# Moving about 400 pieces of a hand-ordered FNet and feed-forward kernel to other places

## The chip, the cores and the metric

The kernel runs on one core of a Trainium2 chip. The time is the device time of one execution in microseconds; smaller is better. The engines are PE (TensorE, matmuls), DVE (VectorE), ACT (ScalarE), POOL (GpSimd) and SP (SyncE, which here only issues DMAs).

## The reference

An FNet mixing layer and a feed-forward layer, each behind a layer norm, over x of 2048 rows and 512 columns in fp32:

```python
def _A_ref(x, dft_seq_re, dft_seq_im, dft_hid_re, dft_hid_im):
    a = jnp.einsum("bsd,ed->bse", x, dft_hid_re)
    b = jnp.einsum("bsd,ed->bse", x, dft_hid_im)
    return jnp.einsum("ts,bse->bte", dft_seq_re, a) - jnp.einsum("ts,bse->bte", dft_seq_im, b)
...
h = x + _A_ref(_layernorm(x, axis=-1), A_dft_seq_re, A_dft_seq_im, A_dft_hid_re, A_dft_hid_im)
h2 = h + _B_ref(_layernorm(h, axis=-1), B_w1, B_w2)
```

where `_B_ref` is `silu(x @ w1) @ w2` with 1792 hidden features.

## The kernel before

**Arithmetic.** Every fp32 product is three matmuls in the fp32r type (`three`, L285 to L287): an operand v is split into a rounded part (`rounded`, L235: an ACT copy to fp32r, names ending in h) and a remainder (L239 and L241: a DVE subtraction, names ending in l). In the tables, `ph` and `pl` are the parts of a page `raw` of the DFT matrix, `S` and `X` those of sums of the normalized x and of x itself, `gth` and `gtl` those of the activations. Large products are done by seven block products instead of eight, so that many block sums are made on DVE, and many banks of PSUM are emptied by ACT copies (`copy_out`: `C` at L536, `p` at L650).

**Stages.** `plain(0, 0)`, `fast(1, 0)`, `mix(0)` make the mixing layer for one half of the output rows, `fast(0, 1)`, `fast(1, 1)`, `mix_fast(1)` for the other; `up` and `down` are the two products of the feed-forward layer. A column sum over all partitions, needed for the second layer norm, is POOL's `partition_all_reduce` (`total`, L952 to L954), eight times in all, each behind two DVE sums of its own; `m01` is one of its results. One kind of block sum over `raw` is made by an accumulating DMA that POOL issues (L702).

**The end.** `down` closes with output blocks `r00`, `r01`, `r10`, `r11` (128 x 1024 each), to which banks of PSUM are added (`add`, L1245) before SP stores them (`store`, L1211). The last two banks are `f5`, added to `r01` and `r11`, and `f4`, of which the first half is added to one half of `r10`; the other half of `r10` was put into bank `f4b` beforehand (L1263), where PE's last matmuls add to it, and is copied out in two pieces, one by DVE (L1287) and one by ACT (L1285), stored by SP and by ACT's own queue (L1288).

**The order.** The program is a list of 1477 events, small functions that issue a few instructions. Each has a place in microseconds, given by `step` and `at` with leads and delays by hand; `program()` adds to the place of event n the number `MOVED[n]`, and sorts:

```python
return sorted(((t + MOVED.get(n, 0.0), at, n, f) for t, at, n, f in events), key=lambda v: v[:3])
```

The kernel issues the events in that order, and on PE, DVE, ACT, POOL and SP each instruction stays behind the one issued before it (`issue_after`, `ORDERED`). So an instruction whose input is late holds up all that stands behind it on its engine. The places are not times at which anything runs; they give only the order. A `Plan` replays the same list ahead and hands out 51 SBUF pages by the order of their last uses, so that another order also gives other pages, and with them other waits of a load for the page that it overwrites.

Of the kernel before, what the change touches and what calls it, by code (L numbers as in the profile page):

```python
# [44 lines left out]
    0: -52.37, 1: -33.2, 2: -38.66, 3: -18.04, 4: -26.92, 5: -20.32, 6: -29.82, 7: -14.98, 8: -9.18, 11: -10.08,  # L45
    12: 25.37, 14: 18.68, 16: 23.49, 21: 2.24, 24: 5.1, 28: 5.71, 31: -2.34, 32: -4.51, 35: 4.85, 36: 5.08, 38: -0.24,
    39: 3.5, 40: 11.88, 41: 1.55, 42: 0.25, 46: 6.79, 53: -4.31, 54: 1.45, 58: -0.74, 59: -9.01, 60: -6.33, 61: -8.84,
    64: -6, 65: -1.09, 66: -2.09, 67: -5.31, 68: -4.92, 71: -10.71, 72: -9.91, 73: -3.53, 74: -2.8, 78: 3.78,
    79: 6.06, 80: 0.77, 81: -13.68, 82: 4.24, 84: -30.43, 85: -17.16, 86: -25.23, 87: -17.93, 88: 2.24, 89: 1.74,
    93: 2.98, 95: -6.14, 96: -2.42, 98: -1.97, 99: -7.61, 100: -1.63, 102: -5.02, 107: -16.33, 110: -10.38,  # L50
    111: -25.35, 112: -9.3, 118: -5.99, 119: -1.79, 122: 1.43, 123: 4.1, 126: -10.19, 127: 0.73, 129: 5.4, 130: 4.42,
    131: -3.95, 134: 0.06, 135: 2.84, 137: -2.02, 139: 1.11, 141: -5.61, 142: 1.4, 145: 2.5, 146: 4.5, 147: 4.57,
    148: 4.6, 149: 3.43, 150: 2.26, 151: 19.19, 152: -7.18, 153: -6.63, 155: 11.15, 156: 11.07, 157: 9.78, 158: 12.14,
    159: 13.16, 160: 16.93, 161: 13.96, 162: -2.9, 163: -3.39, 164: -1.57, 165: -14.91, 166: -17.14, 167: -1.43,
    168: -0.32, 169: -3.29, 170: -12.4, 171: -5.05, 172: -32.94, 173: -31.77, 174: -8.22, 175: -4.04, 176: -5.26,
    179: 0.15, 180: 10.12, 181: 15.11, 182: -25.4, 183: -2.31, 184: -4.6, 186: 1.11, 188: 8.91, 189: 8.76, 190: 7.03,
    191: 5.95, 192: -10.95, 193: -3.24, 194: -7.1, 195: -6.25, 196: -9.27, 197: -18.74, 198: -8.3, 199: -9.45,
    200: -10.15, 201: -10.15, 202: 23.62, 203: 13.92, 204: 13.22, 205: 13.48, 206: 15.71, 207: -25.16, 208: -5.87,
    209: -6.45, 211: -30.57, 212: 4.81, 213: 5.94, 215: 3.47, 216: 4.56, 217: 7.05, 219: -16.42, 221: 2.26,
    223: 10.17, 224: -6.48, 225: -5.63, 226: -3.21, 228: -3.03, 229: 1.98, 233: 6.23, 234: 4.63, 236: -20.67,  # L60
    237: -4.86, 238: -2.92, 240: 13.91, 241: -7.64, 242: -0.78, 243: -2.11, 245: -18.15, 246: 1.78, 247: 1.56,
    249: -6.13, 250: -0.11, 251: 4.03, 253: 7.26, 254: 3.79, 255: 5.2, 257: 2.94, 258: 6.21, 259: 5.94, 260: -5.32,
    261: 0.52, 262: 2.64, 263: -4.66, 265: 4.76, 266: 3.32, 268: 4.67, 269: 3.04, 271: 8.94, 272: 7.88, 273: 0.53,
    274: 5.4, 275: 11.11, 276: -4.5, 278: 7.7, 279: 5.88, 280: 15.06, 282: -4.98, 283: -3.67, 285: -6.12, 286: 0.9,
    288: 2.33, 289: 2.31, 290: 2.16, 291: 2.6, 292: 2.43, 293: -5.69, 295: 6.59, 296: 5.2, 297: 6.85, 299: -1.02,
    302: -1.88, 303: 5.15, 306: 1.26, 307: -5.64, 308: 2.53, 309: 1.36, 310: -1.13, 312: 7.01, 313: 2.51, 314: 3.71,
    315: 2.32, 317: 2.86, 318: 4.16, 320: 2.57, 321: 1.08, 322: 2.71, 324: 2.35, 325: 6.97, 326: 6.39, 327: 7.74,
    329: 2.18, 330: -17.05, 331: -10.08, 332: -6.68, 335: -4.49, 338: 4.22, 339: 6.54, 341: -20.61, 342: -9.19,
    343: 5.09, 344: 5.24, 345: 6.04, 346: 4.03, 347: 2.51, 349: -6.51, 350: -8.89, 351: -7.77, 352: -0.77, 353: 4.15,
    354: -8.39, 355: 4.62, 356: 5.31, 357: 3.14, 358: 1.71, 360: -8.8, 361: -4.61, 362: 0.81, 363: -0.42, 364: 2.41,  # L70
    365: 2.61, 367: -19.81, 368: -19.31, 370: -9.58, 371: -3.37, 372: 3.24, 373: 1.07, 374: 5.51, 375: 6.78,
    376: 13.95, 378: 8.17, 379: 12.62, 380: -2.37, 381: -4.43, 382: -5.31, 383: 9.92, 384: 12.54, 385: -5.3,
    386: 10.75, 387: 3.35, 388: 4.44, 389: 1.23, 392: 31.21, 393: -1.74, 394: -4.65, 395: -5.49, 396: 2.12, 397: 0.45,
    399: 0.6, 400: -4.78, 401: 3.37, 402: -1.34, 403: 3.45, 404: 11.63, 405: 8.49, 406: 2.76, 407: 6.66, 408: -10.79,
    409: -5.26, 410: -16.78, 411: -4.87, 412: -19.75, 413: -6.46, 416: 8.66, 417: 7.28, 418: 6.58, 419: 15.43,
    420: 11.64, 421: 16.66, 422: -28, 423: -3.82, 424: 0.47, 427: 5.11, 428: 6.96, 430: -5.76, 431: -3.41, 432: -4.29,
    434: -24.87, 435: -5.1, 436: 5.45, 439: -3.5, 441: 3.31, 444: 5.76, 445: 3.6, 447: -10.22, 448: 2.95, 449: 2.53,
    451: 1.94, 452: 3.93, 453: 5.93, 455: 11.48, 456: -5.77, 457: 6.32, 458: 6.74, 460: 10.61, 461: 4.86, 462: 6.27,
    464: 5.91, 465: 9.22, 466: 7.05, 468: 0.59, 469: 3.35, 470: 4.72, 474: -1.83, 475: -1.07, 478: -2.17, 480: 1.69,
    481: -0.48, 484: 6, 486: 4.72, 487: 3.83, 488: 5.34, 489: 4.77, 490: 5.95, 491: 5.71, 493: 7.13, 494: 5.75,  # L80
    495: -3.07, 497: 5.65, 498: 5.03, 500: 5.02, 501: 3.02, 503: 5.25, 504: 4.47, 505: 0.13, 506: 1.52, 507: 2.32,
    510: 6.63, 511: 5.94, 512: 11.03, 514: 5.45, 515: 5.04, 517: -0.39, 518: -1.83, 520: 3.53, 521: 1.36, 522: 5.69,
    523: 4.52, 524: 5.7, 525: 2.14, 527: 8.59, 528: 7.15, 529: 5.77, 530: 7.7, 536: 1.31, 539: 9.45, 540: 6.62,
    541: 6.7, 542: 8.33, 544: 9.12, 545: -33.8, 546: 4.76, 547: 1.6, 548: 16.35, 549: -27.35, 550: -9.59, 551: -11.76,
    554: 4.38, 555: 4.21, 558: 3.97, 559: 4.8, 562: 0.83, 563: 3.82, 566: 5.9, 567: 4.31, 568: 4.51, 570: -20.73,
    571: -14.98, 572: -9.8, 575: 2.87, 576: 0.73, 578: -26.34, 579: -16.65, 580: -12.12, 582: 12.19, 583: 5.44,
    584: 2.64, 585: 4.63, 587: -12.47, 589: 2.94, 591: -3.53, 592: -5.23, 593: -2.61, 596: 6.89, 597: 5.63, 600: 5.72,
    601: 3.55, 602: -6.54, 603: -2.43, 604: -1.51, 605: -5.19, 607: -7.33, 608: 6.06, 610: -7.3, 614: 4.59, 615: -5.2,
    616: -5.83, 618: -8.39, 620: 8.96, 621: 7.18, 622: 6.56, 624: 6.01, 625: 3.84, 627: -8.97, 628: 5.64, 632: -4.62,
    633: -5.73, 634: -5.8, 635: -9.76, 637: 6.54, 638: 5.49, 639: 1.47, 642: 3.21, 644: -10.88, 645: -9.35,  # L90
    647: -3.63, 648: -5.58, 649: -12.3, 650: -1.4, 651: -2.57, 652: -19.86, 654: 3.38, 655: 3.83, 656: 6.13,
    659: -10.23, 660: 5, 664: 7.28, 666: 2.38, 668: 4.1, 669: 3.47, 672: -17.88, 673: -27.63, 674: -23.93,
    675: -34.26, 676: -10.49, 678: -14.8, 680: -19.6, 681: -10.83, 683: 4.38, 684: -18.81, 685: 18.83, 687: 1.39,
    688: -0.78, 692: -19.67, 693: -16.11, 694: -13.42, 695: 36.58, 697: 4.07, 698: 4.26, 699: 2.87, 701: 13.95,
    702: 16.83, 703: -4.89, 704: 0.12, 705: -7.59, 706: 0.42, 709: 1.31, 710: -32.96, 713: 26.35, 714: -20.76,
    716: -30.12, 717: -7.52, 719: -2.44, 723: 15.38, 724: -16.97, 728: 5.47, 730: 1.07, 731: 10.4, 732: -3.37,
    733: -0.27, 738: 12.29, 739: 13.87, 740: -42.3, 741: -31.4, 743: 2.11, 746: 4.55, 747: 9.34, 748: 16.67,
    749: 13.34, 750: 20.58, 751: 26.94, 752: 17.9, 753: 22.79, 754: 22.53, 755: 21.55, 756: 21.49, 757: 19.02,
    758: 47, 759: 32.53, 760: 38.11, 761: 39.91, 762: 13.17, 763: 13.96, 764: 16.64, 765: 14.1, 766: 18.58,
    767: 16.64, 768: 11.21, 769: 10.58, 770: 16.25, 771: 13.78, 772: 14.65, 773: 42.57, 774: 29.6, 775: 38.6,  # L100
    777: 5.55, 778: 2.68, 779: 3.67, 780: 2.46, 781: 3.5, 782: 6.91, 783: 22.33, 784: 13.98, 785: 12.14, 786: 12.92,
    787: 18.89, 788: 18.92, 789: 21.01, 790: -23.55, 791: -25.77, 792: 3.41, 793: 1.24, 794: -10.65, 795: -1.97,
    796: 22.62, 797: -5.44, 799: 40.61, 800: 41.64, 801: 29.18, 802: 27.1, 803: 38.77, 804: -41.83, 805: -21.78,
# [1310 lines left out]
```

## Time and profile before

| | us |
|---|---|
| median of 3 runs (lowest, highest) | 677.45 (677.36, 677.74) |
| the profiled execution | 678.98 |
| its span | 677.2 |
| outside its span | 1.8 |
| PE busy in the span | 665.1 (98%) |
| DVE / ACT / POOL busy | 574.9 / 365.3 / 99.5 |
| mean granted TensorE clock | 0.997 |

The profile is one execution. A row of its timeline gives the start, the duration, the engine, the line, the operation, the tiles and, in brackets, how long the engine had been idle just before and what it waited for. Matmuls overlap, so that a matmul of 0.39 us may follow the one before it after 0.23; the distance between two starts, less that pitch, is what PE lost between them. Rows of the view of waits give an engine and line, whom it waited for, and the microseconds in total, the count and the longest.

### The profile page before, as it was taken

How to read it: one execution, taken by the hardware profiler on the slowest of the kernel's cores; microseconds unless marked ns; L12 is line 12 of the kernel's file. 1: busy time of each engine (PE TensorE's matmuls, PEld its weight loads, DVE VectorE, ACT ScalarE, POOL GpSimd, SP SyncE). 2: the span in 40 equal slices, each digit the busy share in tenths (PEclk: the TensorE clock that was granted, in tenths of full speed). 3: DMA queues.
4: the chain of work that ended last, by engine and by line, in shares of the span. 5: the costliest groups of instructions: out<-in, count | busy, mean ns of one | idle time of the engine just before them, and what ended most of it. 6: DMA issues, size and time to landing. Idle time of an engine off the chain costs nothing.

```text
span 677.2 us, 8341 instructions
## 1 busy us (share of the span) xinstructions
PE 665.1 (98%) x2916; PEld 545.8 (81%) x2916; DVE 574.9 (85%) x723; ACT 365.3 (54%) x459; POOL 99.5 (15%) x130
## 2 busy tenths in 40 slices
PE   8999999999999999999999999999999999999996
PEld 5887887888888778888888888888888888888884
DVE  7999999798767899899989997978989765579864
ACT  6979556463444353544554645676544655565500
POOL 0021201112121251213120002442010000000000
PEclk9999999999999999999999999999999999999998
DMA  8978999779699888789999999727998845878602
GB/s 311 394 236 219 291 390 315 240 214 310 233 362 384 308 279 248 224 283 369 321 298 346 389 325 363 276 92 221 328 417 300 348 139 181 310 278 304 226 31 94
DMA packets 61786, 189.59 MB, mean 280 GB/s; under 512 B 6960, under 2 KB 14640, under 8 KB 61744
## 3 DMA queue, kind: packets, MB, share of 16 engines
q1 hardware_dynamic: 46608, 136.33, 56.6%
q0 software_dynamic: 14848, 52.46, 24.2%
q8 instruction: 23, 0.38, 0.2%
q10 hardware_dynamic: 288, 0.26, 0.1%
q14 instruction: 19, 0.16, 0.1%
HBM read 142.88 MB, written 46.15 MB: 279 GB/s over the span
## 4 chain that ended last, share of the span: by engine, by line
PE 85%; DVE 7%; DMA 3%; ACT 3%; issue 1%; DVEq 0%; SPq 0%; ACTq 0%
PE m L286 10%; PE m L285 10%; PE m L287 10%; PE y L285 8%; PE y L287 8%; PE y L286 8%; PE f L287 6%; PE f L285 6%; PE f L286 6%; PE vx L287 3%; PE vx L286 3%; PE vx L285 3%; DVE pl L239 2%; DMA raw<-in_seq 2%; PE c L285 2%; PE c L286 2%
## 5 line engine op out<-in xcount | busy, mean ns | idle before, releaser
L235 ACT ACTIVATE ph<-raw 128x1024 fp32r<-128x1024 f32 x102 | 104.9, 1055 | 88.2 <-DMA raw<-in_seq 16.8
L239 DVE TENSOR_TENSOR pl<-raw,ph 128x1024 fp32r<-128x1024 f32 x92 | 112.4, 1242 | 11.4 <-ACT ph L235 10.6
L286 PE MATMUL m<-pl,S 128*128 128x512 f32 x192 | 75.0, 390 | 0.0
L287 PE MATMUL m<-ph,S 128*128 128x512 f32 x192 | 74.8, 390 | 0.0
L285 PE MATMUL m<-ph,S 128*128 128x512 f32 x192 | 74.8, 389 | 0.0
L285 PE MATMUL f<-gth,wf 128*128 128x512 f32 x161 | 62.7, 389 | 0.0
L287 PE MATMUL f<-gth,wf 128*128 128x512 f32 x161 | 62.7, 389 | 0.0
L286 PE MATMUL f<-gtl,wf 128*128 128x512 f32 x161 | 62.7, 389 | 0.0
L235 ACT ACTIVATE gth<-g 128x1024 fp32r<-128x1024 f32 x42 | 43.3, 1053 | 30.5 <-DVE g L1230 26.5
L239 DVE TENSOR_TENSOR gtl<-g,gth 128x1024 fp32r<-128x1024 f32 x42 | 50.8, 1220 | 10.2 <-ACT gth L235 10.1
L286 PE MATMUL m<-pl,X 128*128 128x512 f32 x144 | 56.4, 392 | 1.3 <-DVE pl L239 1.3
L285 PE MATMUL m<-ph,X 128*128 128x512 f32 x144 | 56.2, 391 | 1.3 <-ACT p L650 1.3
L287 PE MATMUL m<-ph,X 128*128 128x512 f32 x144 | 56.1, 390 | 0.0
L1113 DVE TENSOR_TENSOR g<-vx,g 128x512 f32<-128x512 f32 x42 | 28.8, 687 | 30.3 <-PE vx L287 13.6
L687 DVE TENSOR_TENSOR raw<-raw,raw 128x1024 f32<-128x1024 f32 x36 | 47.7, 1331 | 0.7 <-DMA raw<-in_seq 0.4
L286 PEld LDWEIGHTS m<-pl,S 128*128 128x128 f32 x192 | 36.0, 188 | 7.9 <-DVE pl L239 0.5
L285 PEld LDWEIGHTS m<-ph,S 128*128 128x128 f32 x192 | 36.1, 188 | 7.5
L287 PEld LDWEIGHTS m<-ph,S 128*128 128x128 f32 x192 | 36.0, 188 | 7.4
L1110 ACT ACTIVATE g<-y 128x512 f32<-128x512 f32 x42 | 25.0, 596 | 27.7 <-PE y L287 27.7
L1107 ACT ACTIVATE g<-g 128x512 f32<-128x512 f32 x42 | 26.1, 627 | 17.9 <-DVE g L1113 17.9
L286 PEld LDWEIGHTS f<-gtl,wf 128*128 128x128 f32 x161 | 30.2, 188 | 6.3
L285 PEld LDWEIGHTS f<-gth,wf 128*128 128x128 f32 x161 | 30.2, 188 | 6.2
(334 smaller groups left out, 1582.8 us busy)
## 6 DMA issues: line engine op xcount, KB each, us to landing
raw<-in_seq SPq DMA_DIRECT2D x84, 512.0 KB, 6.1
wf<-wd SPq DMA_DIRECT2D x56, 512.0 KB, 5.6
sf<-sd SPq DMA_DIRECT2D x28, 512.0 KB, 6.3
raw<-in_seq POOLq DMA_DIRECT2D x16, 512.0 KB, 7.2
w<-in_ffn SPq DMA_DIRECT2D x28, 256.0 KB, 7.7
hf<-fd SPq DMA_DIRECT2D x12, 512.0 KB, 6.4
c<-cd SPq DMA_DIRECT2D x8, 512.0 KB, 7.6
h<-in_xT SPq DMA_DIRECT2D x8, 512.0 KB, 7.8
```

Of the source, the lines that this page charges most:

```text
L235: nc.scalar.activation(hi, src, AF.Copy, scale=sign)
L239: nc.vector.tensor_tensor(lo, src, hi, op=ALU.subtract)
L285: nc.tensor.matmul(acc, wh, mh, start=first, stop=False, skip_group_check=on)
L286: nc.tensor.matmul(acc, wh, ml, start=False, stop=False, skip_group_check=on)
L287: nc.tensor.matmul(acc, wl, mh, start=False, stop=last, skip_group_check=on)
L687: nc.vector.tensor_tensor(o, a, b, op=ALU.subtract)
L1107: nc.scalar.activation(g[q, f][:, tau, :], src, AF.Silu)
L1110: nc.scalar.activation(g[q, f][:, tau, :], src, AF.Copy)
L1113: nc.vector.tensor_tensor(g[q, f][:, tau, :], src, g[q, f][:, tau, :], op=ALU.add)
```

## The change

Only the table `MOVED` is another: 378 of its entries are new, gone or changed. The computation and the instructions of each engine are the same ones. The new table is seven lines longer, so that all that follows stands seven lines further down in the changed kernel (L1245 is L1252 there). PE's order stays but for one step of the first stage; on DVE 190 of 720 instructions move by more than three places, 29 by more than fifteen; on ACT 72 of 459 by more than three; on POOL four; on SP, 55 of 305.

```diff
 MOVED = {
...
-    1485: 17.39, 1499: 35.62,
+    1441: -21.66, 1485: 17.39, 1497: 35.87, 1499: 43,
 }
```

**The end, on DVE.** Before, the adds of `r01` and `r11` stand behind the copy from `f4b`:

```order
L1245 TENSOR_TENSOR r11_5348<-r11_5348,p1_5351 128x1024
L1263 COPY f4b_5549<-r10_5314 128x512
L1245 TENSOR_TENSOR r10_5314<-f4_5398,r10_5314 128x512
L1287 COPY r10_5314<-f4b_5549 128x256
L1245 TENSOR_TENSOR r01_5154<-f5_5390,r01_5154 128x1024
L1245 TENSOR_TENSOR r11_5348<-f5_5390,r11_5348 128x1024
```

And in the changed kernel:

```order
L1252 TENSOR_TENSOR r11_5350<-r11_5350,p1_5353 128x1024
L1270 COPY f4b_5549<-r10_5315 128x512
L1252 TENSOR_TENSOR r10_5315<-f4_5399,r10_5315 128x512
L1252 TENSOR_TENSOR r01_5152<-f5_5392,r01_5152 128x1024
L1252 TENSOR_TENSOR r11_5350<-f5_5392,r11_5350 128x1024
L1294 COPY r10_5315<-f4b_5549 128x256
```

The two adds stand ahead of the copy from `f4b`. On SP, the last stores before:

```order
L1211 DMA out_0<-r00_5152 128x1024
L1211 DMA out_0<-r10_5314 128x512
L1288 DMA out_0<-r10_5314 128x256
L1211 DMA out_0<-r01_5154 128x1024
L1211 DMA out_0<-r11_5348 128x1024
```

And in the changed kernel:

```order
L1218 DMA out_0<-r00_5150 128x1024
L1218 DMA out_0<-r10_5315 128x512
L1218 DMA out_0<-r01_5152 128x1024
L1218 DMA out_0<-r11_5350 128x1024
L1295 DMA out_0<-r10_5315 128x256
```

The stores of `r01` and `r11` go ahead of that of the quarter that DVE copies.

**Around 110 us, on ACT.** `Uh_` is the rounded part of a sum for the second feed-forward product, `spare` the dummy operation that loads a function table, `S10` to `S41` roundings of x's sums, `p110` the copies out of a bank that PE needs next. Before:

```order
L235 ACTIVATE ph_1112<-raw10010_992 128x1024
L235 ACTIVATE Uh_1115<-u1_1069 128x1024
L1373 ACT_TABLE_LOAD
L1373 ACTIVATE spare_95<-spare_95 128x1
L397 ACTIVATE S10_1135<-s00_929 128x512
L397 ACTIVATE S20_1137<-s00_929 128x512
L397 ACTIVATE S30_1139<-s01_930 128x512
L650 ACTIVATE p110_1142<-m101_963 128x512 x2
L235 ACTIVATE ph_1159<-raw10110_1132 128x1024
L235 ACTIVATE Vh_1183<-v1_1070 128x1024
```

And in the changed kernel:

```order
L404 ACTIVATE S41_1111<-s11_1071 128x512
L242 ACTIVATE ph_1114<-raw10010_990 128x1024
L1380 ACT_TABLE_LOAD
L1380 ACTIVATE spare_95<-spare_95 128x1
L404 ACTIVATE S10_1132<-s00_758 128x512
L404 ACTIVATE S20_1134<-s00_758 128x512
L404 ACTIVATE S30_1136<-s01_759 128x512
L657 ACTIVATE p110_1138<-m101_959 128x512 x2
L242 ACTIVATE ph_1155<-raw10110_1050 128x1024
L242 ACTIVATE ph_1173<-raw10211_1047 128x1024
L242 ACTIVATE Vh_1183<-v1_1026 128x1024
L242 ACTIVATE Uh_1186<-u1_1025 128x1024
```

`Uh_` goes from ahead of the table load to behind the copies and three more roundings, and `S41` comes in ahead of it.

**Around 230 us, on DVE.** `raw01200`, `raw01201` and `raw01211` are block sums, `hr` the centred rows of the second layer norm. Before:

```order
L969 SCALAR_TENSOR_TENSOR hr000_2045<-m00_1984,h000_1863 128x512 x2
L687 TENSOR_TENSOR raw01200_1990<-raw01201_1988,raw01200_1990 128x1024
L239 TENSOR_TENSOR pl_2017<-raw01111_1944,ph_2016 128x1024
L687 TENSOR_TENSOR raw01201_1988<-raw01211_1992,raw01201_1988 128x1024
L687 TENSOR_TENSOR raw01211_1992<-raw01200_1990,raw01211_1992 128x1024
L239 TENSOR_TENSOR pl_2053<-raw01210_1907,ph_2052 128x1024
L239 TENSOR_TENSOR pl_2069<-raw01310_2050,ph_2068 128x1024
L241 SCALAR_TENSOR_TENSOR pl_2086<-raw01211_1992,ph_2085 128x1024
L969 SCALAR_TENSOR_TENSOR hr001_2114<-m00_1984,h001_1865 128x512 x2
L239 TENSOR_TENSOR pl_2118<-raw01010_2031,ph_2117 128x1024
L239 TENSOR_TENSOR pl_2092<-raw01110_2014,ph_2091 128x1024
```

And in the changed kernel:

```order
L976 SCALAR_TENSOR_TENSOR hr000_2045<-m00_1990,h000_1829 128x512 x2
L246 TENSOR_TENSOR pl_2015<-raw01111_1944,ph_2014 128x1024
L694 TENSOR_TENSOR raw01200_1986<-raw01201_1984,raw01200_1986 128x1024
L694 TENSOR_TENSOR raw01201_1984<-raw01211_1988,raw01201_1984 128x1024
L694 TENSOR_TENSOR raw01211_1988<-raw01200_1986,raw01211_1988 128x1024
L246 TENSOR_TENSOR pl_2050<-raw01210_1909,ph_2049 128x1024
L248 SCALAR_TENSOR_TENSOR pl_2071<-raw01211_1988,ph_2070 128x1024
L976 SCALAR_TENSOR_TENSOR hr001_2093<-m00_1990,h001_1831 128x512 x2
L246 TENSOR_TENSOR pl_2077<-raw01310_2012,ph_2076 128x1024
L246 TENSOR_TENSOR pl_2097<-raw01010_2029,ph_2096 128x1024
L959 TENSOR_TENSOR v00_2117<-sq000_2114,sq001_2100 128x1024
L960 TENSOR_TENSOR v00_2117<-v00_2117 128x512
```

The remainder of `raw01111` goes ahead of three block sums, those of `raw01211` and the centring of `hr001` ahead of that of `raw01310`, and the total `v00` ahead of the remainder of `raw01110`, which is now behind it. On ACT, the roundings of `raw01110` and `raw01211` go ahead of that of `raw01310` in the same way.

**Other moves that the prediction speaks of.** Around 52 us, ACT's copy of the bank `C22` (L536) goes ahead of the roundings S12, S22 and S32 and of the normalization `xc30` that stood ahead of it. Around 280 us, the two DVE sums and POOL's all-reduce for `m01` go about a dozen DVE instructions forward, and on POOL ahead of the accumulating load of `raw01111` and of two stores of `hr`.

163 rows, old and new, of the table MOVED are left out of this document.

## The prediction

> **What bounds the kernel now.** First the page's first part, the busy time of each engine:
>
> ```profile
> PE 665.1 (98%) x2916; PEld 545.8 (81%) x2916; DVE 574.9 (85%) x723; ACT 365.3 (54%) x459; POOL 99.5 (15%) x130
> ```
>
> PE (TensorE) is busy for 665.1 us, 98% of the span. No matmul is added, removed or made shorter by the change, so all that it can win or lose is the rest: the waits of PE, and what stands after its last matmul. The view by windows shows how dense the work is at its densest:
>
> ```profile
> 300.00:400.00 100.00, 100.00 (x442) 82.64 (x441) 96.57 (x108) 56.53 (x61) 16.11 (x21) 1.00 0.99 344
> ```
>
> The columns are PE, PEld, DVE, ACT, POOL, the granted clock, the DMA engines' share and GB/s. Over these 100 us PE starts 442 instructions, one each 0.226 us, without a gap: that is the pitch against which I measure gaps. DVE is busy for 96.57 us and the DMA engines for 0.99 of the time, so this stretch has no spare on three engines.
>
> Then the view of waits, for PE:
>
> ```profile
> PE m L285 <- ACT p L650: 1.3, 1, 1.3
> PE m L286 <- DVE pl L239: 1.3, 2, 0.8
> PE c L484 <- DVE X L460: 1.3, 1, 1.3
> ```
>
> The third stands in the first microseconds, where PE order and inputs are fixed by the first loads. The first two, with a small one below them, lie in the middle; I take them one by one. Last the timeline of the end, on DVE, on ACT's and SP's queues, and the view of DMA issues:
>
> ```profile
> 665.74 0.69 DVE L1245 TENSOR_TENSOR r<-f,r 128x512 f32<-128x512 f32 x1 [1.90 <-PE f L287]
> 670.50 0.42 DVE L1287 COPY r<-f4b 128x256 f32<-128x256 f32 x1 [4.07 <-PE f4b L287]
> 670.84 2.34 DVE L1245 TENSOR_TENSOR r<-f,r 128x1024 f32<-128x1024 f32 x2
> ```
> ```profile
> 671.37 0.35 ACTq L1288 DMA_DIRECT2D out<-r  x1
> ```
> ```profile
> 673.21 0.33 SPq L1211 DMA_DIRECT2D out<-r  x1
> ```
> ```profile
> out<-r SPq DMA_DIRECT2D x2, 512.0 KB, 2.8
> ...
> out<-r ACTq DMA_DIRECT2D x1, 128.0 KB, 2.1
> ```
>
> DVE waits 4.07 us for bank f4b, which PE fills last, and only then makes two sums of 1.2 us that do not need that bank. Their second store leaves SP at 673.21 and lands 2.8 us later, at 676.0; the span ends at 677.2, 1.2 us behind it. Everything after 673.5 is this store.
>
> **The tail: -2.5 us.** The two sums (r01, r11) come to stand behind the row at 665.74 and ahead of the copy from f4b. Their bank f5 is filled ahead of f4, whose first half released that row, so nothing holds them: they run from 666.4 for 2.34 us, to 668.8, inside the 4.07 us of idle time, and the copy still starts at 670.50. Their stores, now ahead of the copy's on SP, leave at about 667.6 and 668.8 and land 2.8 us later, the second at 671.6. The last to land is then ACT's 128 KB store, 671.37 + 2.1 = 673.5 instead of 676.0: 2.5 us. ACT's copy stays behind DVE's; if that store took the 2.8 us of the large ones because they are still moving, the gain is 1.8, and more than 2.5 is not there. I take 2.5, since the large store should have landed about when the small ones begin to move. [...]
>
> **The wait at 54 us: -0.35.** On PE, and on ACT ahead of it:
>
> ```profile
> 53.45 0.39 PE L287 MATMUL c<-ph,X 128*128 128x512 f32 x1
> 54.04 0.50 PE L285 MATMUL c<-ph,X 128*128 128x512 f32 x1 [0.20 <-ACT C L536]
> ```
> ```profile
> 52.03 1.04 ACT L235 ACTIVATE ph<-raw 128x1024 fp32r<-128x1024 f32 x1
> 52.98 1.00 ACT L536 ACTIVATE C<-c 128x1024 f32<-128x1024 f32 x1
> ```
>
> The starts are 0.59 apart, 0.36 over the pitch. The copy that empties the bank (C22) ran behind roundings of x's sums and that ph; it now stands ahead of three of the four roundings of sums and of the xc behind them. Its row has no idle time before it, so it waited for its turn and not for the bank; some 1 us sooner would do, and the 0.36 goes whole. What comes behind it (S12, S22, S32, 1.66 us by the row of three at 110.22 below) feeds later steps of PE; were that cover gone, it would cost as much as is gained. The range is 0 to 0.36.
>
> **The wait at 112 us: -1.4.**
>
> ```profile
> 111.17 0.39 PE L287 MATMUL m<-ph,S 128*128 128x512 f32 x1
> 112.90 0.50 PE L285 MATMUL m<-ph,X 128*128 128x512 f32 x1 [1.35 <-ACT p L650]
> ```
> ```profile
> 107.74 1.06 ACT L235 ACTIVATE Uh<-u 128x1024 fp32r<-128x1024 f32 x1 [1.05 <-DVE u L1176]
> 108.82 1.28 ACT L1373 ACT_TABLE_LOAD   x1
> 110.11 0.20 ACT L1373 ACTIVATE spare<-spare 128x1 f32<-128x1 f32 x1
> 110.22 1.66 ACT L397 ACTIVATE S<-s 128x512 fp32r<-128x512 f32 x3
> 111.79 1.06 ACT L650 ACTIVATE p<-m 128x512 f32<-128x512 f32 x2
> ```
>
> The gap is 1.73 - 0.23 = 1.50. PE waits for a bank that the copies p110 empty, and these end a chain on ACT: Uh (1.06 us, after 1.05 of idle time in which ACT waits for DVE's u), a table load, three roundings, the copies. The change takes Uh out of this chain and puts it nine places further down. Then ACT need not wait for u either: the chain starts up to 1.05 + 1.06 sooner, and the copies come at least 1.06 sooner. So the gain is between 1.06 and the whole 1.50; against the larger, a rounding (S41, a third of the 1.66) now stands ahead of the table load, still inside the 1.05 of idle time. I take 1.4. Uh's readers, a subtraction that moves with it on DVE and a store to DRAM, are not on PE's path here.
>
> **The waits at 233 and 240 us: -1.2.**
>
> ```profile
> 232.81 0.39 PE L285 MATMUL m<-ph,X 128*128 128x512 f32 x1
> 233.73 0.51 PE L286 MATMUL m<-pl,X 128*128 128x512 f32 x1 [0.53 <-DVE pl L239]
> ```
> ```profile
> 239.18 0.42 PE L285 MATMUL m<-ph,X 128*128 128x512 f32 x1
> 240.36 0.50 PE L286 MATMUL m<-pl,X 128*128 128x512 f32 x1 [0.76 <-DVE pl L239]
> ```
> ```profile
> 227.78 1.23 DVE L687 TENSOR_TENSOR raw<-raw,raw 128x1024 f32<-128x1024 f32 x1 [0.43 <-DMA raw<-in_seq]
> ```
> ```profile
> 235.29 1.22 DVE L239 TENSOR_TENSOR pl<-raw,ph 128x1024 fp32r<-128x1024 f32 x1 [1.61 <-ACT ph L235]
> ```
> ```profile
> 234.19 2.96 ACT L235 ACTIVATE ph<-raw 128x1024 fp32r<-128x1024 f32 x3 [8.59 <-DMA raw<-in_seq]
> ```
>
> The gaps are 0.69 and 0.95, 1.64 together. Both come from DVE idle time while ready work is queued behind an instruction that isn't: 0.43 behind a sum that waits for its DMA, 1.61 behind the subtraction that waits for ACT's rounding of raw01310, itself held 8.59 us by a load. In the new order DVE does pl of raw01111 first, ahead of the sums; ACT rounds raw01110 and raw01211 ahead of raw01310; DVE does their pl and hr001 ahead of raw01310's. So 0.43 of the first gap goes, and the 1.61 covers the whole second one. That makes 0.43 + 0.95 = 1.4; but raw01310's load lands when it does, while PE now arrives 1.75 us sooner, so I take 1.2, between 0 and 1.64.
>
> **The rest of the order: +1.0.** Most moves lie where the consumer comes microseconds later, and cost nothing while that cover stands. One does not look free. On POOL and DVE:
>
> ```profile
> 272.30 0.86 POOL L702 DMA_DIRECT2D raw<-in_seq  x1 [3.76 <-DVE pl L241]
> ...
> 285.60 4.06 POOL L954 PARTITION_ALL_REDUCE m<-m  x1 [4.53 <-ACT ph L235]
> ```
> ```profile
> 274.26 3.58 DVE L239 TENSOR_TENSOR pl<-raw,ph 128x1024 fp32r<-128x1024 f32 x3 [1.13 <-ACT ph L235]
> ...
> 285.35 4.40 DVE L239 TENSOR_TENSOR pl<-raw,ph 128x1024 fp32r<-128x1024 f32 x2
> ```
>
> The all-reduce (m01) and the DVE sums that feed it move about a dozen microseconds forward, ahead of POOL's accumulating load of raw01111 (the row at 272.30). While the all-reduce ran, two subtractions took 4.40 us, where three took 3.58 without it (1.19 each): 4.40 - 2.38 = 2.0 us lost on DVE. At the new place, about 271.5, DVE has 1.13 us of idle time that takes up part; the other 0.9 falls on the subtraction that PE needs next, there being no gap on PE and hardly any lead. I take +1.0, between 0 and 2.0. A gain at the old place is not to be had, since PE had no wait there. A rule of the Trainium skill speaks against the move: "SBUF — State Buffer", "Who interferes with whom", has the later of a DVE instruction with two SBUF inputs and a reading GpSimd one blocked until the other is through. By it the second subtraction could only have begun at 289.66 and ended 1.2 later; the trace has it done at 285.35 + 4.40 = 289.75, so the blocking is shorter than the rule's. By the rule the term would be about 1.1 more, +2.1.
>
> **The sum.** -2.5 - 0.35 - 1.4 - 1.2 + 1.0 = -4.45. The profiled execution took 678.98 us with a span of 677.2 and 1.8 outside it; it is 1.5 above the median of 677.45, which I put outside the changed places. So 674.5 for a profiled execution with a span of 672.75, and 677.45 - 4.45 = **673.0** as the median.
>
> **Rivals.**
>
> *Every wait goes and no new one comes.* The gaps sum to 0.36 + 1.50 + 0.69 + 0.95 = 3.50; with the tail 6.0, that is 671.45, and 671.0 if PE's slow restarts after a wait (0.50 instead of 0.39 in the rows above) go too. For it: the all-reduce stalls DVE wherever it stands, and there may be a lead that I undercounted. Chance 0.17.
>
> *The middle is eaten later, the tail stays.* In 300 to 400 us DVE has 3.4 us to spare of 100 and the DMA engines 0.01 of their time. If PE arrives 2 us sooner and DVE or a load does not, PE waits there for what it had won: 677.45 - 2.5 = 674.9, and with some loss on top up to 676.1. Against it: DVE and the queues are held by PE's banks and by pages that PE frees, so they shift with it as long as the order brings nothing forward past a needed item. Chance 0.22.
>
> *A late load: slower.* The median time of such a load, and PE's first matmul that uses raw01111 again after it:
>
> ```profile
> raw<-in_seq POOLq DMA_DIRECT2D x16, 512.0 KB, 7.2
> ```
> ```profile
> 286.54 0.39 PE L285 MATMUL m<-ph,X 128*128 128x512 f32 x1
> ```
>
> POOL works in order, so the accumulating load of raw01111 now waits for the all-reduce, and that for DVE's sums. I put the all-reduce at 271.5 to 275.6, the load's issue at 276 to 276.5; with 7.2 us it lands at 283.5, and rounding (1.06) and subtraction (1.2) are through near 286, just as PE comes to it at 286.54. From there each further microsecond on DVE is one on PE. Where DVE finishes the sums at 278.5 instead of 271.5, the load costs 7 us: 673.0 + 5.8 or more, 678.8 and up, about 680 at 280. It decides from a delay of about 6 us. Against it: the sums stand early on DVE, and need only products that were ready long before. With it counts that pages are freed in another order, so that loads can be held by their page. Chance 0.09.
>
> *The tail does not do what it says*, because the two sums wait for something but f5: then their stores end last as now and 675.5 is left. Nothing in the rows speaks for it. Chance 0.02.
>
> **How the numbers follow.** Forecast 0.50, all gaps gone 0.17, middle eaten 0.22, late load 0.09, no tail 0.02. The time is that of the forecast, 673.0. Its own range is 672.0 to 674.4 by the bounds of the terms. The range of 8 in 10 takes in the two neighbours: 671.0 (all gaps and restarts) to 676.1 (tail at 1.8 and a loss of 0.5). About 0.2%, 1.35 us, is what a measurement of this kernel can tell from no change. Below 676.1 lie the forecast, the first rival, nearly all of the second and the fourth: 0.87. Between 676.1 and 678.8 I put 0.05, slower 0.08.
>
> **What would show it.** Right: DVE's two last adds behind the row of the half add with no wait of 4 us ahead of them; ACT's 128 KB store landing last, about 1.2 us before the span's end; no PE wait on p at 111, on C at 54; the waits on pl near 233 and 240 gone or under 0.4 each; the span's PE end 1.5 to 2.5 sooner than 670.5. A new PE wait on pl near 276, about 1 us, shows the all-reduce's price. Wrong: any PE wait on pl of more than 1 us between 286 and 400, or DVE idle on a DMA there; a last large store that leaves SP behind f4b's.

## The result

The changed kernel takes 676.94 us (median of 14 runs, 675.79 to 678.44), the kernel before, run beside it, 677.72 (14 runs). The ratio is 0.9985, 95% interval 0.9974 to 0.9995: about 1.0 us faster, between 0.3 and 1.8. The forecast was 673.0 with a range of 671.0 to 676.1; the direction was right, the size was not, and the time lies outside the range.

The profiled execution of the changed kernel took 675.96 us with a span of 674.2, 1.0 below its median. That of before, 678.98, was 1.3 above its own. So these two traces lie 3.0 us apart where the kernels lie 1.0 apart, and a second trace of each was taken (below). The first part of the page after, and its view of waits for PE:

```profile
PE 666.1 (99%) x2916; PEld 545.9 (81%) x2916; DVE 576.0 (85%) x723; ACT 364.8 (54%) x459; POOL 99.0 (15%) x130
```
```profile
PE m L292 <- DVE h L790: 1.1, 1, 1.1
PE m L293 <- DVE pl L248: 1.0, 1, 1.0
PE m L293 <- DVE pl L246: 0.4, 1, 0.4
PE c L293 <- DVE pl L246: 0.2, 1, 0.2
```

The waits on `p` and on `C` are gone. Three waits on DVE, of 1.1, 1.0 and 0.4 us, lead the list, and the first, on `h`, is in nothing that I predicted. Where they stand is seen in the view by windows, after first, then the second trace of before (PE is the third number):

```profile
0.00:200.00 200.00, 198.62 (x861) 160.61 (x862) 178.97 (x261) 124.36 (x158) 29.73 (x52) 1.00 0.88 294
200.00:282.00 82.00, 79.48 (x348) 64.83 (x347) 74.27 (x75) 35.05 (x38) 24.72 (x24) 1.00 0.84 280
282.00:480.00 198.00, 198.00 (x873) 163.51 (x873) 180.60 (x224) 116.37 (x148) 42.37 (x50) 1.00 0.85 304
```
```profile
0.00:200.00 200.00, 196.99 (x853) 159.05 (x854) 178.63 (x262) 122.47 (x156) 30.44 (x52) 1.00 0.87 292
200.00:282.00 82.00, 82.00 (x362) 67.36 (x361) 71.82 (x74) 38.96 (x41) 20.70 (x23) 1.00 0.90 303
282.00:480.00 198.00, 198.00 (x874) 163.71 (x873) 184.40 (x226) 115.23 (x147) 46.37 (x51) 1.00 0.85 298
```

Up to 200 us PE is busy 1.63 us longer after, so that much waiting is gone (861 matmuls begun instead of 853). From 200 to 282 it is idle for 2.52 us where before it has no idle time at all. Behind 282 neither has any. What the change wins in the first third it gives back in the next 80 us.

The same can be read matmul by matmul, since PE's order is the same in all the kernels here from matmul 480 on. The table gives the start of the n-th matmul of a trace (counted without 12 dummy matmuls of L1377 at the very start) less its start in the second trace of before; the times in the head are that trace's. The last column is the time from the start of the last matmul to the end of the span. A minus is a lead; a number that rises from one column to the next is time lost between them.

| trace | 480 (118) | 840 (200) | 900 (213) | 1020 (241) | 1200 (282) | last (668) | then |
|---|---|---|---|---|---|---|---|
| before, first trace | 0.18 | 0.18 | 0.18 | 1.85 | 1.85 | 1.92 | 7.14 |
| before, second | 0 | 0 | 0 | 0 | 0 | 0 | 7.15 |
| after, first trace | -1.81 | -1.78 | -0.41 | -0.07 | 1.23 | 1.41 | 4.62 |
| after, second | -1.79 | -1.78 | -0.81 | 1.16 | 2.46 | 2.63 | 4.63 |
| end alone | -0.01 | -0.01 | -0.01 | -0.18 | -0.21 | 0.13 | 4.6 |
| after, `m01` back | -1.98 | -1.96 | -0.73 | 0.38 | 0.35 | 0.52 | 4.6 |
| after, `m01` and `h` back | -2.16 | -2.15 | -2.15 | -0.48 | -0.51 | -0.39 | 4.6 |
| end and Uh alone | -1.55 | 0.10 | 0.10 | 0.56 | 0.53 | 0.53 | 4.6 |

**The end.** DVE, ACT and SP after, and the stores by the view of DMA issues:

```profile
665.23 2.95 DVE L1252 TENSOR_TENSOR r<-f,r 128x512 f32<-128x512 f32 x3 [1.90 <-PE f L294]
669.99 0.42 DVE L1294 COPY r<-f4b 128x256 f32<-128x256 f32 x1 [1.81 <-PE f4b L294]
```
```profile
670.86 0.35 ACTq L1295 DMA_DIRECT2D out<-r  x1
```
```profile
665.95 2.59 SPq L1218 DMA_DIRECT2D out<-r  x3
670.44 0.33 SPq L1295 DMA_DIRECT2D out<-r  x1
```
```profile
out<-r SPq DMA_DIRECT2D x2, 512.0 KB, 2.7
out<-r ACTq DMA_DIRECT2D x1, 128.0 KB, 2.1
```

The two adds stand in one row with the half add and end at 668.2; DVE's wait for `f4b` has shrunk from 4.07 to 1.81. The three stores ahead leave SP by 668.5; the last of them begins at 668.2 and has landed by 671.0. ACT's leaves at 670.86 and lands 2.1 later, at 673.0, and the span ends 1.2 behind that, at 674.2. From the last matmul to the end it is 4.62 us instead of 7.15: 2.5, as predicted.

**At 54 and 112 us.** ACT after, around both places:

```profile
51.18 1.03 ACT L543 ACTIVATE C<-c 128x1024 f32<-128x1024 f32 x1 [1.50 <-PE c L294]
52.10 1.66 ACT L404 ACTIVATE S<-s 128x512 fp32r<-128x512 f32 x3
```
```profile
108.08 1.66 ACT L404 ACTIVATE S<-s 128x512 fp32r<-128x512 f32 x3
109.64 1.07 ACT L657 ACTIVATE p<-m 128x512 f32<-128x512 f32 x2
```

The copy of C22 begins 1.8 us sooner than before's 52.98 and now waits for the bank itself. The copies p110 begin at 109.64 instead of 111.79. PE starts one matmul each 0.227 us past both places.

**At 274 us**, the price that was foreseen. PE, DVE and POOL after:

```profile
273.71 0.39 PE L292 MATMUL m<-ph,S 128*128 128x512 f32 x1
275.09 0.50 PE L293 MATMUL m<-pl,S 128*128 128x512 f32 x1 [0.99 <-DVE pl L248]
```
```profile
267.64 1.22 DVE L959 TENSOR_TENSOR m<-h,h 128x1024 f32<-128x1024 f32 x1
268.89 0.69 DVE L960 TENSOR_TENSOR m<-m 128x512 f32<-128x512 f32 x1
269.50 4.40 DVE L246 TENSOR_TENSOR pl<-raw,ph 128x1024 fp32r<-128x1024 f32 x2
273.82 1.21 DVE L248 SCALAR_TENSOR_TENSOR pl<-raw,ph 128x1024 fp32r<-128x1024 f32 x1
```
```profile
269.75 4.06 POOL L961 PARTITION_ALL_REDUCE m<-m  x1 [6.30 <-DVE m L960]
275.34 0.90 POOL L709 DMA_DIRECT2D raw<-in_seq  x1 [1.52 <-DVE pl L248]
```

Two subtractions beside the all-reduce take 4.40 us; the next, which PE needs, ends at 275.03, and PE starts at 275.09. That is 1.38 after the start ahead, 1.15 over the pitch, and 0.11 more at the restart: the matmul behind a wait takes 0.50 us instead of 0.39, and the next one follows that much later.

**At 209 us**, the wait that was not foreseen. PE and DVE after:

```profile
208.78 0.39 PE L294 MATMUL y<-ph,H11l 128*128 128x512 f32 x1
210.26 0.47 PE L292 MATMUL m<-ph,X 128*128 128x512 f32 x1 [1.09 <-DVE h L790]
```
```profile
208.89 2.36 DVE L790 TENSOR_TENSOR h<-y,h 128x1024 f32<-128x1024 f32 x2 [2.71 <-DMA h<-in_xT]
```

PE waits for a bank that holds a product `y`, which DVE adds to `h`. In the new order DVE's sums of `h000` and `h001` stand ahead of those of `h010` and `h011`. The `h` that they add to is loaded late: DVE waits 2.71 us for it, and the sum that frees PE's bank waits behind.

### The profile page after: what moved, and what is told of

Read it like the earlier page. It is cut to its first block, busy times and chain, and to the rows that moved or that the text cites. A ratio compares the mean times of both kernels' runs of the same rounds, so it can differ in the third digit from the quotient of the medians.

```text
span 674.2 us, 8332 instructions
## 1 busy us (share of the span) xinstructions
PE 666.1 (99%) x2916; PEld 545.9 (81%) x2916; DVE 576.0 (85%) x723; ACT 364.8 (54%) x459; POOL 99.0 (15%) x130
## 4 chain that ended last, share of the span: by engine, by line
PE 63%; DVE 1%; issue 1%; ACT 0%; DVEq 0%
PE f L294 6%; PE f L292 6%; PE f L293 6%; PE m L293 6%; PE m L294 6%; PE m L292 6%; PE y L293 6%; PE y L292 6%; PE y L294 6%; PE vx L292 3%; PE vx L294 3%; PE vx L293 3%; DVE pl L246 1%; PE f4b L294 0%; PE f4b L293 0%
## 5 line engine op out<-in xcount | busy, mean ns | idle before, releaser
L246 DVE TENSOR_TENSOR pl<-raw,ph 128x1024 fp32r<-128x1024 f32 x92 | 116.2, 1285 | 9.4 <-ACT ph L242 8.6
L694 DVE TENSOR_TENSOR raw<-raw,raw 128x1024 f32<-128x1024 f32 x36 | 43.9, 1221 | 0.6
```

The costliest lines, as they stand in the source:

```text
L246: nc.vector.tensor_tensor(lo, src, hi, op=ALU.subtract)
L694: nc.vector.tensor_tensor(o, a, b, op=ALU.subtract)
```

## The experiments

Each edit is to the table `MOVED` alone: some of its entries take the other kernel's value, and one entry (393, below) takes a new one. So every kernel computes the whole result. The edits below show only the entries that differ, put together in a line; `...` stands for those left out. Times are medians; ratios are to the kernel before, run beside it.

**The end alone, and a second trace of before and of after.** Kernel before with the one entry that moves the closing copy behind the adds:

```diff
+    1497: 35.87,
```

> The order of before with one event moved: the two copies out of bank f4b and their stores go behind the last two adds and their stores. Theory: the tail is worth its full 2.5 us in every execution, and the change lost most of that again in the middle. Then about 675.2 us against 677.7 for before, with ACT's 128 KB store landing last, PE's waits in the middle as in before. Rival: the tail is worth much less than its trace (the stores crowd each other or the end has a floor), and the middle of the change is about even: then 676.7 to 677.7.

Measured: 675.4, ratio 0.9968 (0.9951 to 0.9985), 2.2 us, and 4.6 us from last matmul to end. The term of the end is real and stays whole. So the rest of the change, some 377 entries, is worth about 1.2 us on the wrong side (0.9985 less 0.9968; the intervals overlap, so this difference alone is not clear of the noise).

The second traces have no edit.

> The kernel before, unchanged, for a second trace. If the waits at 233 and 240 us hang on when one load lands, they are other than 0.69 and 0.95 here: near 0.1 where the load of raw01310 lands by 232 instead of 234, and the execution is then up to 1.4 us shorter than the first one's 678.98. If they belong to the order, they are the same again.

> The changed kernel, unchanged, for a second trace. The waits at 209 and 274 us should be there again. If the spread of this kernel's times (675.8 to 678.4) comes from the all-reduce's place, the wait at 274 is larger in a longer execution; if it comes from loads, the waits at 209 and 232 to 236 are.

They took 677.07 and 677.27 us. In the second of before the waits at 233 and 240 us, which had cost 0.69 and 0.95, are 0.12 and nothing. PE there:

```profile
232.55 0.39 PE L285 MATMUL m<-ph,X 128*128 128x512 f32 x1
232.90 0.50 PE L286 MATMUL m<-pl,X 128*128 128x512 f32 x1
```

And on ACT, the rounding that waits for the load of raw01310:

```profile
232.35 2.96 ACT L235 ACTIVATE ph<-raw 128x1024 fp32r<-128x1024 f32 x3 [6.93 <-DMA raw<-in_seq]
```

It starts at 232.35 instead of 234.19 (231.88 in the kernel with the end alone, which has no wait there either). The load landed 1.8 us later in the first trace of before than here, with the same order: SP issued it at 224.76 and 224.58 us, and it took 9.3 us there and 7.7 here. Nearly all that sets the first trace apart in the table are the 1.67 us that it loses between matmuls 900 and 1020. In the second trace of after the same place waits:

```profile
233.35 0.50 PE L293 MATMUL m<-pl,X 128*128 128x512 f32 x1 [1.22 <-DVE pl L246]
...
236.96 0.50 PE L293 MATMUL m<-pl,X 128*128 128x512 f32 x1 [0.58 <-DVE pl L246]
```

So the new order there does not take two waits away. Its waits at this place sum to 0.6 and 2.1 us in its two traces; with before's order they are 1.6 in the first trace, and 0.1 in the second and in the kernel with the end alone. How often an execution of before has the late load is not known: its median, 677.72, lies between the two traces (677.07 and 678.98).

**The all-reduce back at its old place.** Changed kernel with:

```diff
-    408: -27.67,
+    408: -10.79,
```

> The changed kernel with one event at before's place: the sums and the all-reduce m01 again behind the accumulating load of raw01111 and the remainders that PE needs next. Theory: PE's wait at 274 us (1.15 us and a restart of 0.1) goes: 676.9 - 1.25 = 675.7. Rival: the wait is due to the remainders' own order on DVE and not to the all-reduce; then the wait at 274 stays and the time is 676.9, or the all-reduce makes a new wait near 286, with the same time.

Measured: 674.6, ratio 0.995 (0.9936 to 0.9964). The wait at 274 us is gone and none takes its place (0.38 and 0.35 in the table at 241 and 282 us). The same two subtractions on DVE, and the one behind them:

```profile
269.00 2.35 DVE L246 TENSOR_TENSOR pl<-raw,ph 128x1024 fp32r<-128x1024 f32 x2
271.27 1.22 DVE L248 SCALAR_TENSOR_TENSOR pl<-raw,ph 128x1024 fp32r<-128x1024 f32 x1
```

They take 2.35 us instead of 4.40. At the old place, 285.95, the all-reduce costs PE nothing, and here DVE hardly anything either. Beside it run a subtraction that began before it and three sums that read a bank of PSUM, each in its usual 1.22 us; the first two:

```profile
285.69 1.22 DVE L246 TENSOR_TENSOR pl<-raw,ph 128x1024 fp32r<-128x1024 f32 x1
286.83 1.22 DVE L717 TENSOR_TENSOR p<-m,p 128x1024 f32<-128x1024 f32 x1
```

By the medians this one entry wins 2.3 us over the changed kernel, more than the 1.3 us lost at 274; by the intervals it is 0.7 to 4.0, so the 1.3 is within them, and no trace shows the rest.

**The sums of `h` back.** First only the two sums of `h000` and `h001`, in the changed kernel:

```diff
-    378: 1.53,
+    378: 8.17,
```

> The changed kernel with one event at before's place: DVE's two sums of h000 and h001, which wait for a late load of x, again behind those of h010 and h011. Theory: PE's wait at 209 us (1.25 us and a restart of 0.1) goes and stays gone: 676.9 - 1.3 = 675.6, and less scatter between runs, since the wait hangs on when a load lands. Rival: PE arrives sooner at 274 us and waits there for DVE instead, 676.9 as the changed kernel.

Measured: 677.22, ratio 0.9999 (0.999 to 1.0008): no gain. Its waits of PE:

```profile
PE m L293 <- DVE pl L246: 1.9, 3, 0.8
...
PE m L292 <- DVE h L790: 0.3, 1, 0.3
```

The wait on `h` shrank to 0.3, since the loads of `h` were left in the new order and DVE still waits 2.03 us for one. Three waits on remainders came at 218, 233 and 236 us (0.70, 0.92 and 0.76 over the pitch). Then the loads of `h` and the other sums too, with the all-reduce back:

```diff
-    376: 10.74, 378: 1.53, 389: 6.11, 391: 2.25, 408: -27.67,
+    376: 13.95, 378: 8.17, 389: 1.23, 408: -10.79,
```

> The changed kernel with m01's all-reduce at before's place, and also the loads of h and their sums on DVE in before's order (h010 and h011 first). Theory (two moves ate the gain): the wait at 209 us goes with its load's turn and 674.6 becomes 673.4. Rival (DVE and the loads between 200 and 240 us are themselves late, as after_h0 showed, where the wait at 209 shrank by 0.8 and others grew at 218, 233 and 236): the wait moves on and the time stays at 674.6.

Measured: 674.13 (673.79 to 675.95), ratio 0.9947 (0.9931 to 0.9964). The wait at 209 us is gone: in the table the lead of 2.15 us is still whole at 213. By 241 it is 0.48. The waits that take it stand at 217 (0.58), 231 (0.35) and 234 us (0.76), each with a restart of 0.11. So the cause of the wait at 209 is shown, and taking it away wins hardly anything: 674.13 against 674.6, within both intervals.

**The early gains by themselves.** Kernel before with the end and all new entries up to a place of 140 (135 entries differ from before in all), among them:

```diff
+    1497: 35.87,
...
-    785: 12.14, 786: 12.92, 789: 21.01, 165: -14.91, 166: -17.14,
+    785: 20.55, 786: 27.12, 789: 30.39, 165: -6.08, 166: -8.22,
```

> The changed order for all events whose places are below 140, before's order for the rest, and the tail. It holds the two removed waits at 54 and 112 us, and neither of the new waits of the changed kernel at 209 and 274 us. Theory (the gain was there and was eaten by new waits): 677.7 - 2.5 - 0.35 - 1.5, about 673.4. Rival (before's profiled execution was one of its slow ones, and its usual execution has not lost those 1.85 us, or the later stages take them back): 675.2, the tail alone.

Measured: 678.45, ratio 1.0008 (1.0 to 1.0017). The waits at 54 and 112 us are gone, but at 143.5 and 153.7 us, where the two orders meet, PE loses 1.83 and 2.34 on remainders. That is the seam's own fault, and the run says nothing of the sum. Then only Uh (its rounding, its subtraction and its stores) and the roundings of x's sums:

```diff
+    1497: 35.87,
-    785: 12.14, 786: 12.92, 789: 21.01, 165: -14.91, 166: -17.14,
+    785: 20.55, 786: 27.12, 789: 30.39, 165: -6.08, 166: -8.22,
```

> The order of before with the tail's event and five more: the rounding Uh with its remainder and store go behind the copies p110 (the place at 112 us), and the roundings S12, S22 and S32 with their remainders go behind ACT's copy of bank C22 (the place at 54 us). Theory (what the change removed in the middle is real, and what it added is what ate it): the waits at 54 and 112 us are gone in the trace and stay gone to the end, 675.4 of the tail alone - 1.85 = 673.5. Rival (from 300 to 410 us DVE and the loads have nothing to spare and take it back): new waits there, 675.4.

Measured: 679.12, ratio 1.0018 (1.0006 to 1.0029). It has a fault of its own too: with those two entries alone, DVE waits for the roundings and PE loses 1.83 at 62 us, and the wait at 54 stays (0.39), since the copy still stands behind a rounding of x and one of `raw` (it begins at 52.91, against 52.82 in the second trace of before). At 137 us it loses another 1.31 on a remainder. So no run shows the wait at 54 us taken away by itself. Without those entries:

```diff
+    1497: 35.87,
-    785: 12.14, 786: 12.92, 789: 21.01,
+    785: 20.55, 786: 27.12, 789: 30.39,
```

> The order of before with the tail's event, and the rounding Uh, its remainder and its store behind the copies p110. Theory (the wait at 112 us is lost time in its own right): it goes and nothing takes its place, 675.3 - 1.6 = 673.7. Rival (as in tail_uh_c, where a wait of 1.3 us stood at 137 us): in before's order DVE has no lead to give there, and a wait on a remainder near 137 us takes most of it back, 675.

Measured: 675.11, ratio 0.9968 (0.9952 to 0.9983), the same ratio as with the end alone. The wait at 112 us is gone (0.06 left). At 133 us, on PE and on DVE:

```profile
133.10 0.39 PE L285 MATMUL m<-ph,X 128*128 128x512 f32 x1
134.64 0.50 PE L286 MATMUL m<-pl,X 128*128 128x512 f32 x1 [1.15 <-DVE pl L239]
```
```profile
133.36 1.23 DVE L239 TENSOR_TENSOR pl<-raw,ph 128x1024 fp32r<-128x1024 f32 x1 [3.00 <-PE m L287]
```

The second trace of before has this subtraction at 133.24, held by ACT; there PE comes to it only at 134.84:

```profile
133.24 1.23 DVE L239 TENSOR_TENSOR pl<-raw,ph 128x1024 fp32r<-128x1024 f32 x1 [1.49 <-ACT ph L235]
```

PE arrives 1.5 us sooner, the remainder comes when it always came, and PE waits for it. What holds it is now PE: a subtraction takes no input from PE, so this is the page that it writes, still read by matmuls. The changed kernel orders this stretch in another way and carries its lead over it (-1.81 at 118 us, -1.78 at 200).

**What holds 200 to 241 us.** All five kernels start from the one with `m01` and `h` back (674.13), and try in turn: two loads at before's places (468, 460); ten steps of ACT and DVE around 230 us at before's places (461, 462, 465, 469, 473, 475, 477, 396, 398, 399); both; POOL's stores of H11 ahead of those of hS10; and that with the ten steps.

```diff
-    468: -5.85, 460: 5.56,
+    468: 0.59, 460: 10.61,
```

> The order of after_m01_h (the changed kernel with m01 and the h loads and sums at before's places) with two loads more at before's places: SP's loads of raw01110 and raw01310 go behind the three that DVE's block sums need. Theory (the sums wait for a load because raw01110's was put ahead of theirs): DVE's wait on a DMA near 227 us goes, and PE's wait at 231 (0.35 and a restart) with it, 674.1 - 0.4 = 673.7; the 0.76 at 234 stays. Rival (the loads land when they do, all being queued on the same engines): no change.

```diff
-    461: 7.28, 462: 7.53, 465: 6.89, ...
+    461: 4.86, 462: 6.27, 465: 9.22, ...
```

> The order of after_m01_h with DVE's and ACT's steps around 230 us at before's places: raw01310's rounding and remainder again ahead of those of raw01211 and raw01110 and of hr001. Theory (the reordering that I priced at -1.2 costs, since PE needs raw01310 first and its load usually lands in time): PE's wait at 234 us (0.76 and a restart) goes, 674.1 - 0.87 = 673.2. Rival (my forecast's reading): the waits at 233 and 240 of the first trace come back, 0.7 to 1.6 longer.

Both edits together:

> Both of the former. Theory: the waits at 231 and 234 go, 672.8, and with them most of the scatter between executions; the fastest of all. Rival: what is left is set by the loads' landing, 673.7 to 674.1.

| kernel | us | ratio (95%) | what PE loses from 200 to 241 us |
|---|---|---|---|
| start | 674.13 | 0.9947 (0.9931 to 0.9964) | 217: 0.58; 231: 0.35; 234: 0.76 |
| two loads | 675.09 | 0.9962 (0.9948 to 0.9976) | 217: 0.61; 231: 0.93; 235: 0.72 |
| ten steps | 675.13 | 0.9969 (0.9955 to 0.9983) | 217: 0.57; 229: 0.68; 232: 0.68 |
| both | 674.03 | 0.9946 (0.993 to 0.9961) | 217: 0.27 and 1.14; 230: 0.25; 233: 0.66 |
| H11 first | 675.58 | 0.9972 (0.9958 to 0.9986) | 217: 0.67 and 1.41; 236: 0.51 |
| H11 first, ten steps | 674.4 | 0.9951 (0.9935 to 0.9967) | 217: 1.41 |

The waits change place and the sum stays between 1.4 and 2.6 us. The new places of the two loads and the new order of the ten steps are not the cause of the loss: with before's own places it is still there.

For the last two there was a theory: SP, which issues the loads of `raw`, waits for a page that the store of H11l still reads. SP's waits from 195 to 225 us in the starting kernel, and POOL's issue of that store:

```profile
SPq L418 <- DMA fd<-H11l: 6.0, 1, 6.0
```
```profile
206.88 0.53 POOL L815 DMA_DIRECT2D fd<-H11l  x1
```
```diff
-    393: 0.94,
+    393: -10.87,
```

> The order of after_m01_h with one event more moved: POOL's two stores of H11 (ready at about 194 us) go ahead of its stores of hS10, which wait for a matmul until 205 to 207. Theory (PE is back at the same time at 241 us in all these orders because SP's loads of the block sums wait for the page of H11l until its store has landed at about 219): that store lands some 6 us or more sooner, the loads with it, and PE's waits at 217, 231 and 234 (0.58, 0.35, 0.76 and restarts) shrink: 674.1 falls to 672.3, and PE is ahead of before by 1.5 us and more at 241 us. Rival (the DMA engines are full from 200 to 232 us, and what comes sooner there only pushes something else back): the waits stay, 674.

And with the ten steps at before's places:

> As h11, with DVE's and ACT's steps around 230 us in before's order (raw01310 ahead of raw01211, hr001 and raw01110). Theory: with loads in time the order that PE needs is the better one, and the wait of 0.76 at 234 goes too: 672.1 - 0.5. Rival: that order makes a wait at 229 us, as it did in dve_230 (0.68), and the time is that of h11 or longer.

The store went out at 195.65, SP's wait for it is gone, and the loss is still there. PE and ACT with H11 first:

```profile
218.09 0.49 PE L292 MATMUL m<-ph,X 128*128 128x512 f32 x1 [0.51 <-ACT ph L242]
219.73 0.50 PE L293 MATMUL m<-pl,X 128*128 128x512 f32 x1 [1.14 <-DVE pl L246]
```
```profile
215.08 2.96 ACT L242 ACTIVATE ph<-raw 128x1024 fp32r<-128x1024 f32 x3 [7.59 <-DMA raw<-in_seq]
```

ACT waits 7.59 us for a load of `raw`; rounding, subtraction and PE's wait follow from it. In the starting kernel it waits 7.21 us at this place:

```profile
212.77 2.01 ACT L242 ACTIVATE ph<-raw 128x1024 fp32r<-128x1024 f32 x2 [7.21 <-DMA raw<-in_seq]
```

So the page that H11l holds is not the cause either. What all six kernels of the table share is this place: ACT waits 5.8 to 8.2 us for a load of `raw`, and PE loses 0.57 us or more at 217. (The later waits, from 229 to 236 us, end in a load in some of the kernels and not in others.) The second trace of before, whose PE comes there 1.5 to 2.2 us later, loses nothing at 217. The DMA engines are full in this stretch; of the second trace of before:

```profile
200.00:208.00 8.00, 8.00 (x37) 6.64 (x36) 3.83 (x4) 3.29 (x4) 1.62 (x4) 1.00 1.01 375
208.00:216.00 8.00, 8.00 (x37) 6.60 (x36) 7.12 (x7) 4.04 (x4) 1.12 (x3) 1.00 1.00 370
216.00:224.00 8.00, 8.00 (x37) 6.63 (x36) 7.60 (x7) 4.11 (x5) 2.94 (x2) 1.00 1.00 376
224.00:232.00 8.00, 8.00 (x37) 6.63 (x36) 7.86 (x8) 1.09 (x2) 2.53 (x3) 1.00 0.95 377
```

A DMA share of 1.01, 1.00, 1.00 and 0.95 over 32 us would explain that a PE which comes 2 us sooner finds its data no sooner. That is argued and not shown: no run moved fewer bytes there, and with H11 first the share from 216 to 224 us was only 0.69, so SP's order and the pages have a part in it. How the loss divides between them stays open.

By the median the fastest are the starting kernel and the one with both (674.13 and 674.03, ratios 0.9947 and 0.9946), within the intervals of the others here. They beat before and the changed kernel (0.9985); what they win over before is mostly the end. What they win over the changed kernel is 2.6 us by the ratios, of which the traces show 1.3 as the all-reduce's place.

## Why the prediction was wrong

| step | predicted | measured |
|---|---|---|
| the end | -2.5 | -2.5 in every trace; -2.2 in time, alone |
| wait at 54 us | -0.35 | gone; but 0.35 and 0.47 at 34 us in after's two traces, where before has no wait |
| wait at 112 us | -1.4 | gone: -1.5, and 0.1 of restart |
| waits at 233 and 240 us | -1.2 | +0.3 and +2.0 |
| all-reduce of `m01` | +1.0 | +1.3 |
| sums of `h` at 209 us | not seen | +1.4 and +1.0 |

The measured column is from PE's starts in the two traces of after against the second of before, so without a trace's own luck at 233 us. The last column of the big table and the ends agree: 1.41 - 2.53 and 2.63 - 2.53 are -1.1 and +0.1; the runs say -1.0.

- **The end** was right by its own steps: the adds run in DVE's idle time, the copy starts when `f4b` is full, and ACT's 128 KB store lands last after 2.1 us.
- **The waits at 54 and 112** went for the reasons given. What failed is the sentence that carries them to the end, against the second rival: DVE and the queues "shift with it". They do not. The 1.8 us of lead at 200 us is nothing or less at 241; even with the sums of `h` back, 2.15 us become 0.48.
- **The waits at 233 and 240** are the step that failed as such. I saw that the profiled execution was 1.5 us above the median and put that "outside the changed places". Nearly all of it lay at exactly these places: a load that landed 1.8 us late in that execution. I counted 1.2 us of gain on waits that two of three traces with before's order don't have, and took it off a median that contains them in part at most. And the new order does not remove such waits: it has 0.6 and 2.1 us of them.
- **The all-reduce** was right in mechanism, with 2.05 us lost on DVE (4.40 less 2.35) and 1.26 on PE (1.15 and the restart). DVE had no idle time ahead of the subtraction in the new order, so the cover was a little smaller than the 1.13 I took. The Trainium skill's rule ("SBUF — State Buffer", "Who interferes with whom") gave +2.1, with the second subtraction beginning only when the all-reduce is through; here it is done at 273.90, 0.1 behind the all-reduce's end at 273.81. The measurement decides, for the shorter blocking.
- **The sums of `h`** stood in the new order and got no term: all other moves were counted at nothing "while that cover stands". That cover was loads of `h`, issued from 202.1 to 203.0 us, which land 5.0 to 8.2 us later.
- **The rivals.** "The middle is eaten later, the tail stays" is what happened: 674.9 with some loss on top up to 676.1. It had the place wrong (DVE's and the DMA engines' 300 to 400 us, where PE loses no more than 0.12 us at any one place in any of these kernels) and the loss too small. The late load of raw01111 did not come: POOL issues it at 275.34, inside my 276, and PE has no wait near 286. Its price was also misread: a load 7 us late, less the 0.8 us between 285.76 and 286.54, costs 6.2 and not 5.8.
- **The range.** "672.0 to 674.4 by the bounds of the terms" is narrower than those bounds: with each term at its best and at its worst the sum runs from 671.45 to 676.6. Even the worst is short of the measured 676.94, since the sums of `h` had no term and the waits at 233 and 240 could only gain.

## What to carry to other kernels

A wait taken away early gives lead, and lead is a gain only if it is still there behind the next stretch in which little is to spare: compare the start of the same matmul in two traces before and behind that stretch. A change behind the last such stretch (here the order of the last stores) kept what it won in every trace. Before a wait of under 2 us that ends in a DMA is priced, take a second trace, above all when the profiled execution is above its median by about as much.

## What was not expected of the hardware

One load, in the same order of the same kernel, let ACT's rounding start at 234.19 in one execution and 232.35 in another. The 14 executions of before beside the changed kernel lie between 677.17 and 679.9, so this spread of 2.7 us is larger than the effect of 378 moved entries, 1.0. And two subtractions that run beside a 4.06 us all-reduce took 4.40 us in before, at 285 us, and in the changed kernel, at 270, where they take 2.35 without it. Yet with its entry back in the changed kernel, at 285.95, the three sums beside it read a bank of PSUM, and nothing was lost. So the price hung on what DVE runs beside the all-reduce, and the lead of the remainders behind it decided whether PE paid. That the bank of PSUM makes the difference is what these rows suggest; no run tried it alone.
